# Reordering the first block of a fused scan, gated MLP and routed MoE kernel

## The chip, the cores and the metric

One core of one Trainium2 chip. The time is device microseconds of a run of the whole program, from the first instruction to the last and the little that lies around them. Three runs of the kernel before give 530.34 to 531.74 us, the median is 531.46 us.

## What is computed

Three layers follow each other. The first is a chunked linear attention with decay: 4 batches of 8 heads, 768 positions, head size 32, state size 16. The reference does it in chunks of 32 positions, cut to what matters:

```python
cum = np.cumsum(log_a_chunk)
M = (C @ B.T) * np.exp(cum_i - cum_j) * causal
y = M @ x + (C @ state) * np.exp(cum_i)
state = np.exp(sum(log_a_chunk)) * state + sum_j(B_j x_j * np.exp(cum_last - cum_j))
```

The second is a gated MLP on the 3072 tokens of 256 features, `(silu(x @ w_gate) * (x @ w_val)) @ w_out` with 1536 hidden features. The third picks one of 8 experts for each token, `relu(x @ w1[e]) @ w2[e]` with 1024 hidden features, scaled by the expert's probability.

## The kernel before

The attention is done in 24 units of 128 positions of one batch, all eight heads at once; four units make a block of 512 tokens, and there are six blocks. A unit u goes through these steps. `load` asks for its two tiles, `xbb` (x and B) and `cbd` (C, block by block on a diagonal). `weigh` multiplies x by a decay (line 278, on POOL or DVE). `scores_mm` makes the new states and the scores on PE (lines 291 and 297). `scores_m` masks the scores on DVE (line 305) and `states` carries the state on DVE and ACT (lines 315 to 327). `values_mm` multiplies on PE (lines 343 and 353). `values_out` scales by the decay `U` on DVE (lines 369 to 372) and rounds to fp32r on ACT (line 374). `values_low` takes the rounding's remainder on DVE (line 380). The decays `U` of a block come from `emit_d` (line 259, a product on POOL for the first two blocks) and `emit_u` (line 270, two products of 512 columns on PE, and line 271, two copies on ACT).

All products of the MLP are in fp32r with a high and a low part of both sides, so three products stand for one. The MLP's weights arrive as 64-bit words in 12 tiles f of 768 KB (`load_w`, line 391, three buffers) and are turned into fp32 by `decode(f, ...)`. Its parts are: 0 and "t", two passes on ACT (lines 403 and 406); "b" and "c", two passes on DVE over 768 columns (lines 412 and 416), which together are part 1; 2, the high part `wh`, on ACT (line 419); 3, the low part `wl`, on DVE or, for tile 0, on POOL (line 421).

The MLP of the first two blocks runs in 24 rounds i. A round makes the gate and the value products of one tile f on PE (`mlp1_mm`, line 441, 12 products `pg` and `pv` of 512 columns), the silu on ACT (line 448), the product on DVE (line 449) and its split into `hh` on ACT (line 455) and `hl` on DVE (line 456). The products with `w_out` (line 469) follow two rounds later. Between them stand the steps of the next units and the decoding of the next weight tile.

`first_block` writes the order of all of this out by hand, and every engine works through its own list in that order (`manual_schedule`). It first issues the loads, prepares the decays, takes units 0 to 3 in a loop (lines 836 to 872), in which PE is also given products that nobody reads (`keep_busy`, line 204), and then starts the rounds. DMAs are issued by SP (the loads) in the order of the text; a load waits on SP until its buffer is free, and what stands behind it waits too. The first MLP product needs units 0 to 3 and weight tile 0; round 1 needs weight tile 1.

The quoted numbers of lines are those of the kernel before.

## Time and profile before

| | |
|---|---|
| runs | 530.34 to 531.74 us, median 531.46 us |
| the profiled execution | 530.17 us, its span 528.4 us |
| PE busy | 505.0 us (96%) |
| DVE busy | 289.1 us (55%) |
| ACT busy | 219.5 us (42%) |
| POOL busy | 105.8 us (20%) |
| the chain that ended last | PE 76%, issue 11%, DVE 4%, POOL 3%, ACT 2%, DMA 1% |
| first MLP product | 24.40 us |

Busy times are sums over the whole span. The timeline has instructions in the order of time with their start, their length, the engine, the line, the tiles and, in brackets, how long the engine had been idle before and what released it. The window view has the busy time of each engine in a stretch. PE rows count passes, of which an fp32 product has two. The last slices of the span hold the loop over further expert tiles.

### The profile page before, as it was taken

To read this page: it belongs to the slowest core of one execution; us is meant where nothing else is said; L and a number is where in the kernel's file an instruction comes from. 1 tells how busy PE (TensorE), PEld (TensorE's weight loads), DVE (VectorE), ACT (ScalarE), POOL (GpSimd) and SP (SyncE) were. 2 spreads that over 40 slices of the span, in tenths; PEclk is the share of its full clock that TensorE was granted. 3 is DMA by queue.
4 is the path that set the end of the run, shared out by engine and by line. 5 is a ranking of instruction groups with operands and counts; after the bars stand their busy time and mean duration, and the time that the engine had idled before them with its cause. 6 is when DMAs were issued, how large, how long until landed. Compare 5 with 4: busy or idle time off the path is not lost.

```text
span 528.4 us, 11243 instructions
## 1 busy us (share of the span) xinstructions
PE 505.0 (96%) x4580; PEld 416.7 (79%) x4580; DVE 289.1 (55%) x631; ACT 219.5 (42%) x403; POOL 105.8 (20%) x127
## 2 busy tenths in 40 slices
PE   6889999999999999999999999999999999999990
PEld 3677787778788778888788778888899989999880
DVE  4998786944554544445444554455466564646320
ACT  4785575434333334233333332434454353534220
POOL 3200000220220130005000224211055426240220
PEclk9999999999999999999999999999999999999995
DMA  8954422011230312012100104234188544521100
GB/s 299 338 183 137 155 80 82 25 49 41 82 32 30 103 15 66 3 47 74 21 2 2 43 1 158 84 121 41 41 105 176 162 130 137 153 104 42 40 22 22
DMA packets 20694, 45.55 MB, mean 86 GB/s; under 512 B 4768, under 2 KB 8352, under 8 KB 20640
## 3 DMA queue, kind: packets, MB, share of 16 engines
q1 hardware_dynamic: 17424, 38.29, 26.2%
q0 software_dynamic: 3072, 6.41, 4.1%
q8 instruction: 37, 0.61, 0.6%
q14 instruction: 17, 0.14, 0.1%
q10 hardware_dynamic: 144, 0.11, 0.1%
HBM read 38.30 MB, written 6.50 MB: 85 GB/s over the span
## 4 chain that ended last, share of the span: by engine, by line
PE 76%; issue 11%; DVE 4%; POOL 3%; ACT 2%; DMA 1%; SPq 0%; POOLq 0%; DVEq 0%; ACTq 0%
PE py L469 19%; PE pg L441 18%; PE pv L441 18%; PE ph L758 7%; PE po L779 6%; PE pt L553 2%; POOL out L793 2%; PE pc L297 2%; PE py L353 1%; PE py L343 1%; PE pc L291 1%; DMA xbb<-in_xbb 1%; PE pu L270 1%; DVE wv L412 1%; PE px L747 1%
## 5 line engine op out<-in xcount | busy, mean ns | idle before, releaser
L441 PE MATMUL pg<-xt,wh 128*128 128x512 f32 x288 | 93.2, 404 | 0.3 <-ACT xt L374 0.2
L441 PE MATMUL pv<-xt,wh 128*128 128x512 f32 x288 | 90.4, 395 | 0.0
L449 DVE TENSOR_TENSOR h<-h,pv 128x512 f32<-128x512 f32 x72 | 49.4, 686 | 66.7 <-PE pv L441 55.6
L456 DVE TENSOR_TENSOR hl<-h,hh 128x512 fp32r<-128x512 f32 x72 | 50.2, 697 | 61.7 <-ACT hh L455 61.5
L758 PE MATMUL ph<-xt,hl 128*128 128x512 f32 x288 | 72.7, 394 | 0.0
L779 PE MATMUL po<-hl,hh 128*128 128x256 f32 x384 | 70.1, 283 | 0.0
L441 PEld LDWEIGHTS pv<-xt,wh 128*128 128x128 f32 x288 | 54.2, 188 | 12.8
L779 PEld LDWEIGHTS po<-hl,hh 128*128 128x128 f32 x384 | 60.3, 188 | 2.1
L455 ACT CAST hh<-h 128x512 fp32r<-128x512 f32 x72 | 44.6, 620 | 40.4 <-DVE h L449 40.4
L441 PEld LDWEIGHTS pg<-xt,wh 128*128 128x128 f32 x288 | 52.1, 188 | 11.6 <-ACT xt L374 0.6
L448 ACT ACTIVATE h<-pg 128x512 f32<-128x512 f32 x72 | 42.7, 593 | 41.7 <-PE pg L441 41.7
L614 POOL DMA_INDIRECT slots<-ids,si x24 | 26.0, 1081 | 168.4 <-DVE si L606 163.6
L758 PEld LDWEIGHTS ph<-xt,hl 128*128 128x128 f32 x288 | 51.7, 188 | 9.2
L469 PE MATMUL py<-hh,wh 128*128 128x512 f32 x144 | 58.7, 407 | 0.0
L441 PE MATMUL pg<-xt,wl 128*128 128x512 f32 x144 | 57.0, 396 | 0.3 <-DVE wl L421 0.3
L469 PE MATMUL py<-hl,wh 128*128 128x512 f32 x144 | 56.9, 395 | 0.0
L469 PE MATMUL py<-hh,wl 128*128 128x512 f32 x144 | 56.8, 394 | 0.0
L441 PE MATMUL pv<-xt,wl 128*128 128x512 f32 x144 | 56.8, 394 | 0.0
L779 PE MATMUL po<-hl,hl 128*128 128x256 f32 x192 | 53.9, 281 | 0.2 <-DVE hl L767 0.2
L767 DVE SCALAR_TENSOR_TENSOR hl<-ph,hh 128x512 fp32r<-128x512 f32 x48 | 33.0, 688 | 31.8 <-ACT hh L766 30.8
L766 ACT ACTIVATE hh<-ph 128x512 fp32r<-128x512 f32 x48 | 28.8, 600 | 41.4 <-PE ph L758 24.3
L779 PEld LDWEIGHTS po<-hl,hl 128*128 128x128 f32 x192 | 36.1, 188 | 0.4 <-DVE hl L767 0.4
(140 smaller groups left out, 669.6 us busy)
## 6 DMA issues: line engine op xcount, KB each, us to landing
eraw<-in_ew SPq DMA_DIRECT2D x24, 512.0 KB
wraw<-in_mw SPq DMA_DIRECT2D x12, 768.0 KB
xbb<-in_xbb SPq DMA_DIRECT2D x24, 256.0 KB
cbd<-in_cbd SPq DMA_DIRECT2D x24, 256.0 KB
yd<-yr SPq DMA_DIRECT2D x6, 528.0 KB
slots<-ids,si POOLq DMA_INDIRECT x24
xg<-yd,idx POOLq DMA_INDIRECT x24
out<-ob,idx POOLq DMA_INDIRECT x24
```

The source lines that it names most:

```text
L297: nc.tensor.matmul(out=r["pc"][g][32 * q:32 * q + 32, 0:256], lhsT=r["bt"][k, 32 * q:32 * q + 32], rhs=r["c"][k, q // 2].rearrange("p h i ...
L441: nc.tensor.matmul(out=t, lhsT=w[:, f, o:o + 128], rhs=xt[:, xp, k, cs], start=n == 0, stop=n == 5)
L448: nc.scalar.activation(out=h, in_=p[0], func=AF.Silu)
L449: nc.vector.tensor_tensor(out=h, in0=h, in1=p[1], op=ALU.mult)
L455: nc.scalar.copy(out=hh, in_=h)
L456: e.tensor_tensor(out=hl, in0=h, in1=hh.bitcast(F32), op=ALU.subtract)
L469: nc.tensor.matmul(out=yb[b][d][:, c:c + m], lhsT=w[:, f, o:o + 128], rhs=h, start=first and n == 0, stop=last and n == 2, skip_group_chec ...
L614: i = nc.gpsimd.indirect_dma_start(out=slots[0:E * upto], out_offset=bass.IndirectOffsetOnAxis(ap=si[:, s:s + 1], axis=0), in_=ids[g][:, o ...
L758: nc.tensor.matmul(out=p, lhsT=self.hl[:, w, o:o + 128], rhs=self.xt[:, xp, k], start=n == 0, stop=n == 5)
L766: nc.scalar.activation(out=hh, in_=p, func=AF.Relu)
L767: nc.vector.scalar_tensor_tensor(out=hl, in0=p, scalar=0.0, in1=hh.bitcast(F32), op0=ALU.max, op1=ALU.subtract)
L779: nc.tensor.matmul(out=self.po[s // 2][:, s % 2], lhsT=h[:, q], rhs=self.hl[:, w, o:o + DM], start=f == 0 and n == 0 and s % 2 == 0, stop= ...
```

## The change

Only `first_block`, `load` and part 3 of `decode` change. `load` can be issued by another engine, and part 3 can be divided over two engines by columns. In `first_block`:

- the small decay product `d2` is made before the constants of `setup_ones`, and `emit_d(0)` stands ahead of `weigh(1)` on POOL;
- `load(3)` moves from the first loads to ACT's queue, `load_w(1)` from there to the end of unit 1, `load_w(2)` and `load_w(3)` to units 2 and 3;
- `emit_u(1)` moves from unit 0 to unit 2; the products that nobody reads are 2, 2, 4 and 4 instead of 0, 4, 4 and 6 after the four units;
- the parts of `decode(0)` move one unit later; its low part is done in unit 3, 512 columns on DVE and 256 on POOL, instead of in unit 1 with all 768 on POOL;
- `decode(1)` keeps its ACT passes 0 and "t" in units 2 and 3, and its DVE passes and the high part move behind `scores_m(4)` and `states(4)`;
- `weigh(6)` on DVE moves from the head of round 0 to just before it.

The number of products of each line of PE stays as it was, but for line 204, which has 12 instead of 14.

```diff
--- before.py
+++ after.py
@@ -157,17 +157,17 @@
     v_t = {}
     s_t = {}
 
-    def load(u):
+    def load(u, e=nc.sync):
         if u >= NU or u in raw:
             return
         r = {}
         xbb = ap_.tile([128, 512], F32, name="xbb", tag="xbb", bufs=4)
-        nc.sync.dma_start(out=xbb, in_=I["xbb"][:, u])
+        e.dma_start(out=xbb, in_=I["xbb"][:, u])
         r["x"] = xbb[:, 0:DM].rearrange("k (h d) -> k h d", h=8)
         r["b"] = xbb[:, DM:DM + 128]
         r["bt"] = xbb[:, DM + 128:]
         r["c"] = ap_.tile([128, 2, 4, 64], F32, name="cbd", tag="cbd", bufs=4)
-        nc.sync.dma_start(out=r["c"].rearrange("p r h i -> p (r h i)"), in_=I["cbd"][:, u])
+        e.dma_start(out=r["c"].rearrange("p r h i -> p (r h i)"), in_=I["cbd"][:, u])
         raw[u] = r
 
     def setup_loads():
@@ -418,8 +418,10 @@
             elif part == 2:
                 nc.scalar.copy(out=wh[:, f], in_=wv_t[f].bitcast(F32))
             else:
-                low.tensor_tensor(out=wl[:, f], in0=wv_t.pop(f).bitcast(F32), in1=wh[:, f].bitcast(F32),
-                                  op=ALU.subtract)
+                v = wv_t.pop(f)
+                for e, k in ((low, slice(0, 768)),) if low is nc.vector else low:
+                    e.tensor_tensor(out=wl[:, f, k], in0=v[:, k].bitcast(F32), in1=wh[:, f, k].bitcast(F32),
+                                    op=ALU.subtract)
 
 
     HALF = NF // 2
@@ -812,29 +814,30 @@
         nc.sync.dma_start(out=at0[:, 2:], in_=I["at"][:, 2:])
         load(2)
         load_w(0)
-        load(3)
-        load_w(1)
         setup_ln(0, 2)
         setup_decay(0, 2)
         setup_cum(0, 1)
         weigh(0, nc.vector)
         scores_mm(0)
         cum_split(0, 1)
+        p = cum_ends_d(0, 1)
         setup_ones()
+        d = emit_d(0)
         weigh(1, nc.gpsimd)
-        d = emit_d(0)
-        p = cum_ends(0, 1, cum_ends_d(0, 1))
+        p = cum_ends(0, 1, p)
         scores_m(0)
         cum_store(0, 1, p)
         states(0)
         emit_u(0, d)
         cum_pairs(1, 8)
         setup_ln(2, NBLK)
-        decode(0, 0)
+        load(3, nc.scalar)
         d = emit_d(1)
         weigh(2, nc.gpsimd)
         for u in range(4):
             scores_mm(u + 1)
+            if u == 2:
+                emit_u(1, d)
             values_mm(u)
             if u == 1:
                 setup_decay(2, NBLK)
@@ -842,36 +845,38 @@
             if u < 3:
                 scores_m(u + 1)
                 states(u + 1)
-            if u in (0, 2):
-                decode(u // 2, "t")
+            if u == 2:
+                decode(1, 0)
             values_out(u)
             if u == 0:
-                emit_u(1, d)
+                decode(0, 0, "t")
+            if u == 1:
                 decode(0, "b")
-            if u == 1:
+            if u == 2:
                 decode(0, "c")
-            if u == 2:
-                decode(1, "b")
-            keep_busy((0, 4, 4, 6)[u])
+            if u == 3:
+                decode(1, "t")
+                silu_first()
+            keep_busy((2, 2, 4, 4)[u])
             values_low(u)
             load(u + 4)
             if u == 0:
                 weigh(3, nc.gpsimd)
             if u == 1:
+                load_w(1)
+                weigh(4, nc.gpsimd)
+            if u == 2:
                 load_w(2)
+                weigh(5, nc.gpsimd)
+                decode(0, 2)
+            if u == 3:
+                decode(0, 3, low=((nc.vector, slice(0, 512)), (nc.gpsimd, slice(512, 768))))
                 load_w(3)
                 nc.sync.dma_start(out=c2, in_=I["cst"][:, C1:C_END])
-                weigh(4, nc.gpsimd)
-                decode(0, 2)
-                decode(0, 3, low=nc.gpsimd)
-                decode(1, 0)
-            if u == 2:
-                decode(1, "c")
-                silu_first()
-                decode(1, 2)
-                weigh(5, nc.gpsimd)
         scores_m(4)
         states(4)
+        decode(1, 1, 2)
+        weigh(6, nc.vector)
         decode(1, 3)
         decode(2, 0, "t")
         load_w(4)
@@ -883,7 +888,7 @@
             b, f = q % 2, f + HALF * (q // 2)
             u = units.get(i)
             w = todo.get(i, NF)
-            if i + 1 in units and units[i + 1] > 4:
+            if i + 1 in units and units[i + 1] > 5:
                 weigh(units[i + 1] + 1, nc.vector if i < 16 else nc.gpsimd)
             if u == 7:
                 mlp1_down(*late.pop(0))
```

The rows below are as the built programs have them: engine by engine, line, operation, output and inputs, shape of the output.

POOL, from its first own row. `xw` is the weighed x of a unit, `du` the input to a block's decays `U`, `wl` the low part of weight tile 0. Before:

```order
L278 TENSOR_TENSOR xw<-xbb,W 128x256
L259 TENSOR_TENSOR du<-er,c_69 128x512 x2
L278 TENSOR_TENSOR xw<-xbb,W 128x256 x3
L421 TENSOR_TENSOR wl<-wv,wh 128x768
L278 TENSOR_TENSOR xw<-xbb,W 128x256
```

After:

```order
L259 TENSOR_TENSOR du<-er,c_69 128x512
L278 TENSOR_TENSOR xw<-xbb,W 128x256
L259 TENSOR_TENSOR du<-er,c_69 128x512
L278 TENSOR_TENSOR xw<-xbb,W 128x256 x4
L423 TENSOR_TENSOR wl<-wv,wh 128x256
```

The first `du` now stands ahead of the first `xw`, and the low part is a third as wide and the last of these.

DVE, from the third unit's last steps to the first rounds. `wv` is a weight tile's bits (L412 is "b", L416 is "c"), `y` and `z` a unit's values, `xt` its remainder, `mt` the masked scores, `sv` and `se` the states. Before, from "b" of tile 1 on:

```order
L412 SCALAR_TENSOR_TENSOR wv<-ha,wv 128x768
L380 TENSOR_TENSOR xt<-y_422,xt 128x2x128
L416 SCALAR_TENSOR_TENSOR wv<-wraw,wv 128x768
L369 TENSOR_TENSOR y_497<-py,U 128x192
L370 TENSOR_TENSOR z_498<-py,U 128x128
L371 TENSOR_TENSOR y_497<-py,U 128x64
L372 TENSOR_TENSOR y_497<-y_497,z_498 128x128
L380 TENSOR_TENSOR xt<-y_497,xt 128x2x128
L305 TENSOR_TENSOR mt<-pc,c_69 128x256 x2
L321 SCALAR_TENSOR_TENSOR sv<-se,eb,pc 128x64
L324 SCALAR_TENSOR_TENSOR se<-sv,eb,pc 128x64
L421 TENSOR_TENSOR wl<-wv,wh 128x768
```

After, from the fourth unit's remainder on:

```order
L380 TENSOR_TENSOR xt<-y_486,xt 128x2x128
L423 TENSOR_TENSOR wl<-wv,wh 128x512
L305 TENSOR_TENSOR mt<-pc,c_69 128x256 x2
L321 SCALAR_TENSOR_TENSOR sv<-se,eb,pc 128x64
L324 SCALAR_TENSOR_TENSOR se<-sv,eb,pc 128x64
L412 SCALAR_TENSOR_TENSOR wv<-ha,wv 128x768
L416 SCALAR_TENSOR_TENSOR wv<-wraw,wv 128x768
L278 TENSOR_TENSOR xw<-xbb,W 128x256
L423 TENSOR_TENSOR wl<-wv,wh 128x768
```

"b" and "c" of tile 1 stand behind `mt`, `sv` and `se` of the fifth unit, and 512 columns of tile 0's low part stand ahead of them. Ahead of `y_486` there is one such pass now, "c" of tile 0.

SP, the loads from the first weight tile on. Before:

```order
L391 DMA wraw<-in_mw 128x1536
L165 DMA xbb<-in_xbb 128x512
L170 DMA cbd<-in_cbd 128x512
L391 DMA wraw<-in_mw 128x1536
L165 DMA xbb<-in_xbb 128x512
L170 DMA cbd<-in_cbd 128x512
```

After:

```order
L391 DMA wraw<-in_mw 128x1536
L165 DMA xbb<-in_xbb 128x512
L170 DMA cbd<-in_cbd 128x512
L165 DMA xbb<-in_xbb 128x512
L170 DMA cbd<-in_cbd 128x512
L391 DMA wraw<-in_mw 128x1536
```

Before, the two loads behind the first weight tile are unit 3; after, they are units 4 and 5, and weight tile 1 stands behind both.

## Rows read from the trace of the kernel before

**Rows 1.** Windows: length; busy of PE, PEld, DVE, ACT, POOL; PE clock; DMA; GB/s.

```profile
28.00:32.00 4.00, 4.00 (x92) 3.09 (x76) 3.85 (x8) 3.45 (x7) 0.00 (x0) 1.00 0.32 72
32.00:36.00 4.00, 2.55 (x101) 2.15 (x101) 3.95 (x8) 2.30 (x5) 0.00 (x0) 1.00 0.67 264
60.00:80.00 20.00, 20.00 (x89) 16.21 (x88) 15.63 (x28) 15.12 (x29) 0.00 (x0) 1.00 0.34 106
```

**Rows 2.** Waits of PE over the whole span: total, times, longest.

```profile
PE pc L291 <- DVE mt L305: 1.5, 1, 1.5
PE pc L297 <- issue: 0.9, 1, 0.9
```

**Rows 3.** The chain that ended last, 50 to 60 us.

```profile
52.47 0.97 DVE wl L421
53.48 1.19 PE pg L441 x4
54.67 1.40 PE pv L441 x6
```

**Rows 4.** Timeline, the start: POOL, DVE and PE up to unit 1's scores.

```profile
5.32 0.30 DVE L226 TENSOR_TENSOR er<-er,eh 128x132 f32<-128x132 f32 x1
...
6.61 0.61 POOL L278 TENSOR_TENSOR xw<-xbb,W 128x256 f32<-128x256 f32 x1 [6.17 <-DMA xbb<-in_xbb]
...
7.18 2.17 POOL L259 TENSOR_TENSOR du<-er,c 128x512 fp32r<-128x512 f32 x2
...
8.27 1.22 PE L270 MATMUL pu<-du,r 128*128 128x512 f32 x2 [1.60 <-POOL du L259]
...
9.43 0.47 PE L291 MATMUL pc<-xw,xbb 64*32 64x64 f32 x16
```

**Rows 5.** Timeline of PE: scores of units 2 to 4, first product, later scores.

```profile
12.57 0.47 PE L291 MATMUL pc<-xw,xbb 64*32 64x64 f32 x16
...
16.37 1.16 PE L204 MATMUL pi<-r 128*128 128x512 f32 x4
...
19.99 0.34 PE L291 MATMUL pc<-xw,xbb 64*32 64x64 f32 x16
...
24.40 0.96 PE L441 MATMUL pg<-xt,wh 128*128 128x512 f32 x2 [0.21 <-ACT xt L374]
...
33.76 0.28 PE L291 MATMUL pc<-xw,xbb 64*32 64x64 f32 x7 [1.45 <-DVE mt L305]
```

**Rows 6.** Timeline of DVE, 20 to 28 us.

```profile
20.10 0.52 DVE L372 TENSOR_TENSOR y<-y,z 128x128 f32<-128x128 f32 x1
20.70 1.22 DVE L412 SCALAR_TENSOR_TENSOR wv<-ha,wv 128x768 int32<-128x768 int32 x1
...
22.17 0.94 DVE L416 SCALAR_TENSOR_TENSOR wv<-wraw,wv 128x768 int32<-128x768 int32 x1
...
23.64 0.27 DVE L372 TENSOR_TENSOR y<-y,z 128x128 f32<-128x128 f32 x1
24.38 0.42 DVE L380 TENSOR_TENSOR xt<-y,xt 128x256 fp32r<-128x256 f32 x1 [0.47 <-ACT xt L374]
...
25.89 0.95 DVE L421 TENSOR_TENSOR wl<-wv,wh 128x768 fp32r<-128x768 f32 x1
26.76 0.42 DVE L278 TENSOR_TENSOR xw<-xbb,W 128x256 f32<-128x256 f32 x1
27.68 0.96 DVE L412 SCALAR_TENSOR_TENSOR wv<-ha,wv 128x768 int32<-128x768 int32 x1 [0.50 <-ACT wv L406]
```

**Rows 7.** Timeline: SP, ACT and POOL on the weight tiles.

```profile
4.51 0.43 SPq L391 DMA_DIRECT2D wraw<-in_mw  x1
...
11.24 0.92 ACT L403 ACTIVATE ha<-wraw 128x768 f32<-128x768 f32 x1 [0.75 <-DMA wraw<-in_mw]
...
18.62 1.85 POOL L421 TENSOR_TENSOR wl<-wv,wh 128x768 fp32r<-128x768 f32 x1 [2.75 <-ACT wh L419]
...
23.15 0.83 ACT L419 CAST wh<-wv 128x768 fp32r<-128x768 f32 x1 [0.57 <-DVE wv L416]
```

## The prediction

> **What bounds the kernel now.** I read the page first: PE is busy for 96% of the span and holds 76% of the chain that ended last, so only a moment at which PE waits can be worth anything. The windows say where there are such moments: from 60 us on PE is busy for all 20 us of 20, while from 32 to 36 us it has 2.55 of 4 and DVE 3.95 of 4 [rows 1]. The waits of PE name one large one behind the start of the MLP, 1.45 us for DVE's masked scores [rows 2, 5]. The chain of work runs on DVE once more up to 53.48 us, and from there on PE alone [rows 3]. So the time is fixed by two things: when the first MLP product starts (24.40 us, [rows 5]), and whether DVE and ACT, which decode weights and serve the units beside it, then keep up. What comes out at 33.76 us, where PE is released by DVE, moves the rest of the program one for one. I therefore sum the change in two stretches: to the first product, and from there to that release.
>
> **Stretch one: to the first product.**
>
> 1. The decays first. Now POOL takes unit 1's weighing at 6.61 us, after waiting for its load, and only then the two decay products, 2.17 us for both; PE gets the first at 8.27 us after 1.60 us of idle time [rows 4]. The decays' input is ready when DVE is done with it, at 5.32 + 0.30 = 5.62 us. With the decay first on POOL it is done at about 5.65 + 1.08 = 6.73, and PE starts at about 6.75: 1.52 us earlier. The weighing behind it ends at 7.35 and is needed when the two 512-column products are through, 6.75 + 1.15 = 7.9; it is hidden by half a microsecond. Moving the small product d2 ahead of the constants gains nothing: PE is at scores until 6.3 anyway.
> 2. Units 1 to 2. The scores of unit 1 start at 9.43 - 1.52 = 7.9. Up to the scores of unit 2 the distance is 12.57 - 9.43 = 3.14 us now [rows 4, 5]; the two 512-column products in it (block 1's decays) give way to two others of the same size, so these start at 11.05.
> 3. Units 2 to 4. From there to unit 4's scores it is 19.99 - 12.57 = 7.42 us [rows 5]. Two of the four unread products go (1.16 us for four, so 0.58), the two of block 1's decays come (0.58): zero. Unit 4's scores start at 18.5.
> 4. To the first product it is 24.40 - 19.99 = 4.41 us now. In it DVE does "b" and "c" of tile 1, 1.22 and 0.94 us, ahead of unit 3's values [rows 6]; in their place it has one pass, "c" of tile 0 (0.95). That takes 1.2 us out: 3.2. The two unread products fewer are hidden, since PE waits for DVE and ACT there. First product at 21.7, **2.7 us earlier**.
> 5. What hides the rest. Unit 3 is asked for by ACT, two issues of some 0.4 us each behind its logarithm, at about 9 us. Now the load leaves SP earlier but stands behind weight tile 0, which took from 4.51 until 11.2 to land [rows 7]. I take it to land at about 12.5; unit 3's scores, which need it, cannot start before 11.05 + 3.14 = 14.2, so it has 1.7 us to spare. Tile 1's load now stands on SP behind unit 5's, which waits for unit 1's values; it is issued at about 13.8. ACT wants it at about 18, ahead of unit 2's rounding on the same queue. The nearest row has 6.7 us from issue to landing for such a tile, with a full queue around it; 768 KB at the 264 GB/s of a window [rows 1] are 3.0 us. Between these I take 4.2 us, nearer the low end because few loads stand ahead by then, so that it lands at 18.0 and costs nothing, and keep 20.5 as the late end.
> 6. Tile 0's low part on two engines: POOL's 1.85 us become about 0.62 for a third of the columns, beginning as soon as the high part is done; DVE gets 0.95 x 512 / 768 = 0.63 us in stretch two.
>
> [...] DVE's last step on a unit's values took 0.52 us at 20.10 and 0.27 at 23.64 [rows 6]; at 20.10 POOL was at its low part, which ran until 20.47 [rows 7]. [...]
>
> **Stretch two: from the first product to the release of PE by DVE.** Now DVE takes 33.76 - 24.38 = 9.38 us from unit 3's remainder to that release [rows 5, 6], all but idle only for 0.50 us. Behind the change it does the same list and in addition:
>
> 7. 0.63 us of tile 0's low part (point 6).
> 8. "b" and "c" of tile 1, 0.96 and 0.95 us without disturbance: 1.9 us.
> 9. A wait. Tile 1's high part is made by ACT (0.83 us) after "c", and the low part on DVE needs it; before, it had long been there. Unit 6's weighing (0.42) lies beside it: +0.4 us. Then tile 2's two ACT passes (0.92 and about 0.9) come behind the high part, and DVE has the low part (0.95) beside 1.8 us of them: 0.85 us of waiting instead of 0.50: +0.35 us.
>
> So it takes 9.4 + 0.63 + 1.9 + 0.75 = 12.7 us: **3.3 us longer**. Starting from 21.7 it ends at 34.4, 0.65 us later than now. PE sees this as follows: round 1 starts at about 29, as now, because round 0's silu on ACT stands behind tile 1's high part and tile 2's passes, and PE idles before it for some 2.5 us; the next scores wait again for DVE.
>
> **Sum.** -2.7 + 3.3 = +0.6 to +0.7 us on the profiled execution of 530.17 us, so 530.8. The median of the runs is 1.29 us above that execution; on it the forecast is 531.46 + 0.65, rounded to **532.1 us**: no change that a measurement could tell, 0.3% being 1.6 us. Unknown costs: PE's wait of 0.9 us for nothing the profile shows [rows 2] may not come back, and PE's faster clock may come earlier. [...] If the upper level comes 2 us sooner, half of these is won, -1.0. At the other end stand the late landing of point 5 (+2.0 at most) and the 0.6 us of the port.
>
> **Rivals.**
>
> - *DVE has room after all (faster).* If stretch two hid its additions beside PE's work, the 2.7 us would stay but for DVE's 0.63: 531.46 - 2.1 = 529.4 us. For it: DVE is busy for only 55% of the span. Against: it has 3.95 us of 4 where it matters [rows 1], and the 1.45 us of PE's wait are there before anything is added. It decides from 1.0 us of slack upwards; the trace shows 0.50.
> - *Weight tile 1 is late (slower).* Its place on SP is behind two loads that wait for PE and for their buffers. ACT then stands before the tile's first pass, and unit 2's rounding, unit 2's remainder on DVE and unit 3's values stand behind it. Each microsecond of landing after about 18.2 is one on both stretches. At the 6.7 us of tile 0 it lands at 20.5: +2.3 on top of the forecast, 534.4 us. It counts as slower from 19.2 us on. For it: that is the one row that times such a load. Against: the DMA queue is emptier by then.
> - *The clock falls (slower).* PE idles for some 2.5 us before round 1 and again before the next scores. In the trace it came through a wait of 1.45 us at 33.76 without losing its clock, since six products take 1.40 us afterwards [rows 3]. At the lower level each six would take 2.8, and one round (two sixes) behind the idle time would cost 2.8 us: 534.9. [...]
> - *It does nothing.* The counts of PE's lines are the same but for two unread products, so no product that counts is saved; all is order. If stretch two's waits of point 9 fall into time that is idle anyway, gain and loss cancel, and the time is 531.5.
>
> **Chances.** The forecast has 0.69, DVE with room 0.10, the late tile 0.14, the fallen clock 0.03, nothing 0.04. Same is 0.69 + 0.04 = 0.73, slower 0.14 + 0.03 = 0.17, faster 0.10. The range: from 532.1 down by the 1.9 us of the unknowns on that side, to some 530.0; upwards by 2.0, the late tile's most likely part, to 534.0.
>
> **What would show it.** Right: a first PE decay product near 6.75 us, a first MLP product between 21 and 22.5, a PE wait of 2 us or more ahead of round 1, then the scores released by DVE near 34.4, and the same stretch from there to the end. Wrong: round 1 starting 4.6 us behind round 0 as now; ACT waiting for a weight tile's DMA near 18 us; six products taking 2.8 us after 29 us; or any difference that comes up behind 55 us.

## The result and the profile after

| | median us | runs | lowest to highest |
|---|---|---|---|
| before, same series | 530.75 | 8 | 530.34 to 531.74 |
| after | 533.32 | 8 | 532.19 to 535.73 |

The ratio is 1.0052, with a 95% interval of 1.0039 to 1.0066: 2.6 us slower. That is inside the forecast's range, but outside the 0.3% that it called no change. The profiled executions are 530.17 us before and 532.19 us after (the fastest of its eight), with spans of 528.4 and 530.0 us.

First PE's timeline, whose rows answer to [rows 4, 5]. The columns are as there: start, duration, engine, line, operation, tiles, count, and in brackets the idle time ahead and what ended it.

```profile
6.95 0.40 PE L238 MATMUL pe<-d,r 128*128 128x32 f32 x1 [0.46 <-DVE r L215]
7.25 1.19 PE L270 MATMUL pu<-du,r 128*128 128x512 f32 x2
...
11.51 0.47 PE L291 MATMUL pc<-xw,xbb 64*32 64x64 f32 x16
...
17.80 0.34 PE L291 MATMUL pc<-xw,xbb 64*32 64x64 f32 x16
19.59 0.67 PE L297 MATMUL pc<-cbd,xbb 64*32 64x256 f32 x16 [1.45 <-issue]
...
22.34 0.95 PE L443 MATMUL pg<-xt,wh 128*128 128x512 f32 x2 [0.27 <-ACT xt L374]
...
29.37 0.72 PE L443 MATMUL pg<-xt,wh 128*128 128x512 f32 x2 [1.97 <-ACT h L450]
...
34.96 0.28 PE L291 MATMUL pc<-xw,xbb 64*32 64x64 f32 x7 [1.58 <-DVE mt L305]
```

The reader sees the trade of the forecast. The first MLP product comes 24.40 - 22.34 = 2.06 us earlier. PE then idles 1.97 us ahead of round 1, which it did not do before, and the release of PE by DVE comes 34.96 - 33.76 = 1.20 us later. The first stretch ends 0.64 us later than its forecast of 21.7, and it has two waits nobody counted, at 6.5 and at 18.1 us.

The timelines of the other engines say what stands behind the waits (rows for [rows 4, 6, 7]):

```profile
5.83 1.07 DVE L215 CAST r<-c 128x128 fp32r<-128x128 f32 x1
...
5.77 1.04 POOL L259 TENSOR_TENSOR du<-er,c 128x512 fp32r<-128x512 f32 x1 [5.34 <-DVE er L226]
...
13.69 0.42 SPq L391 DMA_DIRECT2D wraw<-in_mw  x1
...
18.76 0.89 ACT L403 ACTIVATE ha<-wraw 128x768 f32<-128x768 f32 x1 [1.40 <-DMA wraw<-in_mw]
...
19.98 0.43 DVE L380 TENSOR_TENSOR xt<-y,xt 128x256 fp32r<-128x256 f32 x1 [1.02 <-ACT xt L374]
20.97 0.36 DVE L369 TENSOR_TENSOR y<-py,U 128x192 f32<-128x192 f32 x1 [0.57 <-PE py L353]
...
22.67 0.69 DVE L423 TENSOR_TENSOR wl<-wv,wh 128x512 fp32r<-128x512 f32 x1
...
24.44 0.95 DVE L412 SCALAR_TENSOR_TENSOR wv<-ha,wv 128x768 int32<-128x768 int32 x1
25.43 0.96 DVE L416 SCALAR_TENSOR_TENSOR wv<-wraw,wv 128x768 int32<-128x768 int32 x1
...
27.28 0.96 DVE L423 TENSOR_TENSOR wl<-wv,wh 128x768 fp32r<-128x768 f32 x1 [0.56 <-ACT wh L419]
28.87 0.96 DVE L412 SCALAR_TENSOR_TENSOR wv<-ha,wv 128x768 int32<-128x768 int32 x1 [0.62 <-ACT wv L406]
```

Weight tile 1, asked for at 13.69, is there 5.0 us later, and ACT waits 1.40 us for it. DVE's remainder of unit 2 at 19.98 then waits 1.02 us, because ACT's rounding stands behind the tile. It is not the tile that sets the first product here, though: at 20.97 DVE stands 0.57 us more, for PE's values of unit 3, which come behind PE's wait at 18.1 us. Behind the first product DVE does the three additions of the forecast's points 6 to 8 (0.69, 0.95 and 0.96 us) and stops twice for ACT.

In one cut, from the first product to the release DVE's list took 33.76 - 24.40 = 9.36 us before and 34.96 - 22.34 = 12.62 after. It got 3.26 us longer for a start that was 2.06 us earlier. That is the +1.20. Some 0.4 us more come up behind the release: from there to the end of the span it is 494.6 us before and 495.0 after. They come among the expert tiles, from some 420 us on, and in no other profile: the twelve below have 494.4 to 494.7, so the release does move the rest one for one. Another 0.4 us lie around the span: 530.17 - 528.4 = 1.8 us before, 532.19 - 530.0 = 2.2 after.

Not explained by this profile is that the median is +2.57 us and the runs spread over 3.5 us, where before's spread over 1.4.

### The profile page after: what moved, and what is told of

It reads as the page before. It is cut to its first block, busy times and chain, and to the rows that moved or that the text cites. A ratio compares the mean times of both kernels' runs of the same rounds, so it can differ in the third digit from the quotient of the medians.

```text
span 530.0 us, 11238 instructions
## 1 busy us (share of the span) xinstructions
PE 505.1 (95%) x4578; PEld 416.1 (79%) x4578; DVE 290.6 (55%) x632; ACT 219.5 (41%) x403; POOL 104.9 (20%) x127
## 4 chain that ended last, share of the span: by engine, by line
PE 77%; issue 11%; DVE 5%; POOL 2%; ACT 2%; DMA 1%; SPq 0%; POOLq 0%; ACTq 0%
PE py L471 19%; PE pg L443 18%; PE pv L443 18%; PE ph L760 7%; PE po L781 6%; PE pt L555 2%; PE pc L297 2%; POOL out L795 2%; PE py L353 1%; PE py L343 1%; PE pc L291 1%; DVE wv L412 1%; PE pu L270 1%; PE px L749 1%; POOL xg L719 1%
## 5 line engine op out<-in xcount | busy, mean ns | idle before, releaser
L443 PEld LDWEIGHTS pv<-xt,wh 128*128 128x128 f32 x288 | 54.1, 188 | 13.5 <-DVE h L451 0.9
```

What stands on the lines that cost most here:

```text
L443: nc.tensor.matmul(out=t, lhsT=w[:, f, o:o + 128], rhs=xt[:, xp, k, cs], start=n == 0, stop=n == 5)
```

## Theories

- **A.** DVE's list behind the first product sets the release; its additions and its waits for ACT are the loss.
- **B.** Weight tile 1 lands too late. What the median shows beyond the profile is a tile that usually lands later than in the profiled run.
- **C.** TensorE's clock falls in PE's new idle time, and that is most of the loss.

All versions ran in five rounds beside before, whose median in the four series was 530.41, 530.38, 530.36 and 530.36 us. This table holds what the profiles of all of them say; "stretch two" is the release less the first product, the last column the median less before's of the same series.

| version | tile 1 landed | first product | release | stretch two | median |
|---|---|---|---|---|---|
| before | 14.4 | 24.40 | 33.76 | 9.36 | 0 |
| after | 18.7 | 22.34 | 34.96 | 12.62 | +2.57 |
| a_again | 20.0 | 23.64 | 35.98 | 12.34 | +2.61 |
| decode_first | 20.6 | 23.99 | 35.97 | 11.98 | +1.88 |
| low_pool | 19.7 | 24.15 | 36.17 | 12.02 | +2.26 |
| tile_early | 13.1 | 22.46 | 35.05 | 12.59 | +2.04 |
| old_loads | 14.7 | 23.13 | 35.73 | 12.60 | +2.07 |
| old_first | 14.3 | 22.90 | 34.88 | 11.98 | +1.48 |
| no_bc | 21.1 | 24.47 | 35.74 | 11.27 | +0.73 |
| act_tile | 17.7 | 23.66 | 35.84 | 12.18 | +1.67 |
| loads_act | 17.9 | 24.30 | 33.66 | 9.36 | +0.50 |
| du_only | 14.1 | 24.02 | 33.37 | 9.35 | -0.38 |
| du_all | 14.1 | 24.12 | 32.91 | 8.79 | -0.98 |
| unit3_sp | 19.3 | 22.75 | 35.35 | 12.60 | +2.30 |

## Experiments

### The changed kernel once more (a_again)

No edit.

> The changed kernel once more, with another trace. Theory A (DVE's list: the work put behind the fifth unit's states, and the waits for ACT around it, outweigh the earlier start): again 0.3 to 0.6% slower than before, PE released by DVE's masked scores at 34.5 to 35.5 us, and every six products behind 29 us in 1.4 us. Theory B (weight tile 1 lands late): the release moves one for one with the landing of tile 1, which ACT waits for. Theory C (PE's clock falls in the idle time ahead of round 1 in some runs): six products take 2.8 us somewhere between 29 and 34 us if this trace is of such a run.

533.02 us (532.59 to 534.47), ratio 1.0049 (1.0031 to 1.0067). Its profile is of a more usual run than the first. First its timeline:

```profile
19.98 0.92 ACT L403 ACTIVATE ha<-wraw 128x768 f32<-128x768 f32 x1 [2.46 <-DMA wraw<-in_mw]
...
20.36 0.67 PE L297 MATMUL pc<-cbd,xbb 64*32 64x256 f32 x16 [2.29 <-issue]
...
21.86 0.36 DVE L369 TENSOR_TENSOR y<-py,U 128x192 f32<-128x192 f32 x1 [0.21 <-PE py L353]
...
23.64 1.05 PE L443 MATMUL pg<-xt,wh 128*128 128x512 f32 x2
...
32.50 1.22 PE L443 MATMUL pv<-xt,wh 128*128 128x512 f32 x2 [0.22 <-DVE h L451]
...
35.98 0.25 PE L291 MATMUL pc<-xw,xbb 64*32 64x64 f32 x3 [0.42 <-DVE mt L305]
```

And its windows, with the columns of [rows 1], the granted clock in front of the last two:

```profile
22.00:24.00 2.00, 2.00 (x5) 1.39 (x6) 1.53 (x6) 1.08 (x2) 0.73 (x1) 0.50 0.59 180
...
26.00:28.00 2.00, 2.00 (x56) 1.48 (x58) 1.71 (x3) 0.70 (x2) 0.00 (x0) 1.00 0.63 239
...
32.00:34.00 2.00, 1.78 (x5) 1.21 (x5) 2.00 (x6) 1.44 (x3) 0.00 (x0) 0.50 0.54 129
```

The tile took 6.4 us from its issue at 13.60 and ACT waited 2.46 us, so it is late as B has it. But again DVE stood last for PE's values, 0.21 us: PE, which had waited 2.29 us at 18.07, set the first product, with the tile close behind. That product is 1.3 us later than in the first profile, and stretch two is not longer. C is seen too, twice: at 22 and at 32 us the granted clock is at 0.50, and two products at 32.50 took 1.22 us, for 0.73 in the first profile. The first fall, in the unread products, held the first product some 0.3 us longer but not DVE: counted from DVE's remainder of unit 3 (23.35) the release comes 12.63 us later, as in the first profile (12.64 from 22.32). The second fall moved nothing either: PE's wait ahead of the release is 0.42 us in place of 1.58, so the slower products went into a wait for DVE that was there anyway.

### Tile 1's decode ahead of unit 4's masked scores (decode_first)

```diff
+        decode(1, 1, 2)
         scores_m(4)
         states(4)
-        decode(1, 1, 2)
```

> Undoes one part: both DVE passes of tile 1 and its high part stand ahead of the fifth unit's masked scores and states again, all else as changed. Theory A: DVE's two waits for ACT (0.56 and 0.62 us) shrink, round 1 starts 0.6 to 0.9 us sooner, PE is released at 33.9 to 34.4, and the time is 0.6 to 1.0 us below the changed kernel's, 532.3 to 532.7. Theory B: the tile is as late as before, no change, 533.3. Theory C: PE idles about 0.7 us less; the same or up to 2 us less.

532.29 us (530.70 to 532.76), ratio 1.0027 (1.0017 to 1.0038), 0.7 us below the changed kernel in the same series. Stretch two has 11.98 us in place of 12.6. Unit 4's masked scores and states now lie where DVE waited 0.56 us for the high part, and the next wait is shorter:

```profile
28.59 0.95 DVE L423 TENSOR_TENSOR wl<-wv,wh 128x768 fp32r<-128x768 f32 x1
29.89 0.96 DVE L412 SCALAR_TENSOR_TENSOR wv<-ha,wv 128x768 int32<-128x768 int32 x1 [0.35 <-ACT wv L406]
```

A step that only reorders DVE's list gives its microseconds back, as A says. The release itself, 35.97, is not at the forecast 33.9 to 34.4, because the tile landed at 20.6 in this profile and the first product came at 23.99.

### The low part on POOL alone (low_pool)

```diff
-                decode(0, 3, low=((nc.vector, slice(0, 512)), (nc.gpsimd, slice(512, 768))))
+                decode(0, 3, low=((nc.gpsimd, slice(0, 768)),))
```

> Undoes one part: tile 0's low part is all on POOL again (768 columns), all else as changed. Theory A: DVE's list is 0.69 us shorter, PE is released 0.6 us sooner, 532.7. The first product's third partner may come as late as 22.7, which costs nothing as the release counts. Theory B and C: no change, 533.3, within 0.3 us.

532.67 us (532.52 to 533.31), ratio 1.0040 (1.0026 to 1.0055). Two rows of the timeline stand side by side:

```profile
21.71 1.80 POOL L423 TENSOR_TENSOR wl<-wv,wh 128x768 fp32r<-128x768 f32 x1 [4.06 <-ACT wh L419]
...
21.87 1.79 DVE L372 TENSOR_TENSOR y<-y,z 128x128 f32<-128x128 f32 x1
```

A DVE step that takes 0.27 us undisturbed [rows 6] took 1.79 us and ended 0.15 us behind POOL's. So the split avoids most of a stop of 1.5 us on DVE at the price of 0.69 us of DVE work (stretch two is 12.02 here), and comes out about even: of the 0.35 us by which this median is below the changed kernel's in the same series, 0.3 lie around the span (below). The time is the 532.7 that A gave, but not by A's way: the release, 36.17, came later and not 0.6 us sooner.

### Tile 1 asked for early (tile_early)

```diff
             values_low(u)
+            if u == 0:
+                load_w(1)
             load(u + 4)
...
-                load_w(1)
                 weigh(4, nc.gpsimd)
```

> Undoes one part: weight tile 1 is asked for at the end of unit 0 instead of unit 1, ahead of the fifth unit's loads. Theory A: ACT's wait of 1.40 us for the tile goes, and with it up to 1.0 us of DVE's idle time at 19 us, but PE's own wait in unit 4's scores holds the first product; 0 to 0.6 us less than the changed kernel, 532.7 to 533.3. Theory B: the whole loss goes, 530.7 or below. Theory C: no change.

532.45 us (531.60 to 533.75), ratio 1.0034 (1.0020 to 1.0048). The queue took the issue at 4.96 us, and the tile landed at 13.08. ACT no longer waits for it. But unit 3 landed at 14.85, and POOL waited for that:

```profile
14.98 1.57 POOL L278 TENSOR_TENSOR xw<-xbb,W 128x256 f32<-128x256 f32 x2 [5.70 <-DMA xbb<-in_xbb]
```

Release and stretch two are those of the changed kernel's first profile. The median is 0.6 us below a_again's; what a late unit 3 took back of B's worth this run can't tell, since the late tile was exchanged for it.

### Both loads in their old place (old_loads, old_first)

```diff
         load_w(0)
+        load(3)
+        load_w(1)
...
-        load(3, nc.scalar)
...
-                load_w(1)
                 weigh(4, nc.gpsimd)
```

old_first has the edit of decode_first besides.

> The changed kernel with the loads of unit 3 and of weight tile 1 back in their old places, on SP's queue right behind weight tile 0; all else as changed. Theory A with B (DVE's added work sets the release of PE, at 35.0 us where the tile is there in time; what the runs without a profile lose beyond that is the tile landing 5 to 7 us after its late issue): the tile lands near 14.5, ACT waits for no load, unit 3 is there before its scores, release 34.6 to 35.1, and the time is 531.7 to 532.1, with a small spread as before's. B alone (the late tile is all of the loss): the time of before, 530.5. C (a clock that falls in PE's idle time is most of the loss): 533 as the changed kernel, with its spread.

> The two old loads, and tile 1's second decode ahead of unit 4's masked scores and states. A with B: DVE's two passes on the tile and ACT's high part come earlier, so DVE no longer waits 0.56 us for the high part, and round 1 comes sooner: release 33.9 to 34.5, time 530.9 to 531.4, the best of the series so far, but not faster than before by what can be told. B alone: 530.5, as the run with the old loads. C: PE idles less ahead of round 1, 532.0.

532.45 us (531.72 to 532.77), ratio 1.0032 (1.0022 to 1.0041), and 531.86 us (531.12 to 532.02), ratio 1.0019 (1.0011 to 1.0028). The spread is before's again. tile_early, with the tile early and unit 3 late, had a spread of 2.15 us, so the wide spread is not tile 1's late landing alone. Against a_again and decode_first, their likes with late loads, the two gain 0.5 and 0.4 us. The second, whose release of 34.88 and time came later than its forecast, is the best version that has all of the change's other parts, and still 1.5 us above before, 0.4 of it around the span.

The time of old_loads is above what A with B gave it, and its first product is 0.8 us later than after's although no load is late. Some 0.3 us of that is DVE's last step on unit 3's values, which took 0.55 us beside POOL's part of the low part and 0.28 in after. The rest is PE. The timeline:

```profile
15.64 0.69 PE L193 MATMUL pe<-c,at 128*128 128x132 f32 x4 [1.85 <-DVE y L372]
...
21.76 0.74 POOL L423 TENSOR_TENSOR wl<-wv,wh 128x256 fp32r<-128x256 f32 x1 [2.37 <-ACT wh L419]
...
22.10 0.55 DVE L372 TENSOR_TENSOR y<-y,z 128x128 f32<-128x128 f32 x1
...
23.13 0.95 PE L443 MATMUL pg<-xt,wh 128*128 128x512 f32 x2 [0.55 <-ACT xt L374]
...
35.73 0.28 PE L291 MATMUL pc<-xw,xbb 64*32 64x64 f32 x7 [1.59 <-DVE mt L305]
```

The releaser that is named is not the likely one: DVE's L372 ended at 15.13, and after does the same products without a wait for it. Other records fit better: the view of the DMA queues lists, in a window, packets of the kind "instruction" (queue, kind: packets, MB, share of 16 engines). First old_loads, 12 to 14.5 us; then after, 9.5 to 12 us; then before, 13 to 14.5 us:

```profile
q1 hardware_dynamic: 393, 0.96, 99.4%
q8 instruction: 1, 0.02, 2.3%
```

```profile
q10 hardware_dynamic: 241, 0.45, 49.4%
q1 hardware_dynamic: 175, 0.40, 43.0%
q8 instruction: 1, 0.02, 4.1%
```

```profile
q1 hardware_dynamic: 292, 0.56, 98.2%
q8 instruction: 1, 0.02, 3.9%
```

By the packet records this one packet of 16 KB (before's queue q8 has 37 of the kind over the span, 0.61 MB) ran 13.12 to 14.05 us in old_loads, 13.40 to 14.34 in before and 10.12 to 11.77 in after, and the next one 17.30 to 18.27 in after. PE started again 1.59 us behind the end of the first in old_loads, 1.56 in before (its row "15.90 ... [0.85 <-issue]"), and 1.32 us behind the second in after: its wait of 1.45 us at 18.14. The fourteen profiles have such stops at two places of PE's program alone: at the products of L186 and L193 near 14 us, and at L297 of unit 4's scores near 19. In all fourteen the restart of such a stop is 1.3 to 1.6 us behind a packet's end, so these packets are read here as PE's own code and called code packets below; no view names the engine that they are for. The view counts them in the same share of 16 engines as the loads of q1 and q10 (4.1% in after's window). The first of them starts at 12.8 to 13.4 us in the five profiles with both loads in their old place on SP, and at 10.1 to 12.2 in the nine others. Full engines alone do not explain that: in after's window they are at some 96% too, half of it from ACT's queue (q10). What the packet waits for no run shows.

### Less work on DVE (no_bc)

```diff
-        decode(1, 1, 2)
+        decode(1, 2)
         weigh(6, nc.vector)
```

> The changed kernel without DVE's two passes 'b' and 'c' of weight tile 1 (its exponent and sign are left out, so that part of the first MLP's weights is not the reference's); 1.9 us of DVE work less between the first product and the release, nothing else. A: the release falls by 1.5 to 1.9 us against the changed kernel with the same landing of the tile, to 33.1 to 33.6, and the time is 531.0 to 531.5 or less. B (the late tile holds all up through ACT): under 0.5 us of gain, 532.5. C: PE's idle time ahead of round 1 gets shorter by about 1.5 us; if that saves the clock, more than 1.9 us are won and the spread shrinks.

The run leaves out the passes "b" and "c" of tile 1. 531.11 us (530.30 to 532.70), ratio 1.0014 (1.0003 to 1.0025): 1.9 us below the changed kernel's 533.02 of the series before, as A said. It was a run with a very late tile that was profiled:

```profile
21.11 0.90 ACT L403 ACTIVATE ha<-wraw 128x768 f32<-128x768 f32 x1 [3.38 <-DMA wraw<-in_mw]
...
24.47 0.96 PE L443 MATMUL pg<-xt,wh 128*128 128x512 f32 x2 [1.87 <-ACT xt L374]
...
27.98 0.96 DVE L423 TENSOR_TENSOR wl<-wv,wh 128x768 fp32r<-128x768 f32 x1 [1.00 <-ACT wh L419]
```

So its release, 35.74, does not show the gain; stretch two, 11.27 us, does: 1.35 us shorter, and 0.44 us of the rest went into a longer wait for ACT (1.00 against 0.56).

### Tile 1 asked for by ACT (act_tile)

```diff
         load(3, nc.scalar)
+        load_w(1, nc.scalar)
...
-                load_w(1)
                 weigh(4, nc.gpsimd)
```

> The changed kernel with one thing moved: weight tile 1 is asked for by ACT, right behind unit 3, at about 9.7 us in place of 13.7. It tells the tile's landing from the load of PE's code: every run so far in which unit 3 and tile 1 were asked for early (on SP, at 5 to 6 us) shows the first 16 KB load of PE's code ending near 14.0 and PE standing still until 1.3 to 1.6 us after that, and every run in which they were asked for late shows it ending by 11.8 and PE not standing there. A with B and with the code load as a second reason of the time at which the first MLP product starts: the tile lands by 16.5, ACT does not wait for it, the code load ends by 12.5 and PE has no idle time near 14, first product 22.3 (2.1 earlier than before), release 35.0 (1.2 later), time 531.6 to 532.0 with a small spread. If the code load has nothing to do with the loads ahead of it: PE idles near 14 as with the old loads, first product 23.1, release 35.7, 532.4. C: 533 with the spread of the changed kernel.

532.03 us (531.82 to 532.47), ratio 1.0030 (1.0019 to 1.0042). The first code packet ended at 11.70 us and PE did not stand at 14, as expected if the code waits behind SP's loads. (What is said there of every run has one exception: in decode_first the packet ended at 12.64 and PE stood 0.67 us at 13.5.) The rest of the forecast failed in the profile: the tile took 7.5 us and landed at 17.66, and the second code packet ended at 18.89, behind its loads; its timeline and two of its windows:

```profile
20.26 0.68 PE L297 MATMUL pc<-cbd,xbb 64*32 64x256 f32 x16 [2.23 <-issue]
...
21.88 0.36 DVE L369 TENSOR_TENSOR y<-py,U 128x192 f32<-128x192 f32 x1 [2.07 <-PE py L353]
...
35.84 0.28 PE L291 MATMUL pc<-xw,xbb 64*32 64x64 f32 x7 [0.65 <-DVE mt L305]
```

```profile
22.00:24.00 2.00, 2.00 (x5) 1.54 (x6) 1.53 (x6) 1.20 (x2) 0.00 (x0) 0.50 0.67 220
...
32.00:34.00 2.00, 2.00 (x6) 1.36 (x5) 1.97 (x6) 1.44 (x4) 0.00 (x0) 0.50 0.66 135
```

ACT's wait for the tile is all but gone (0.23 us), and the first product is no earlier than a_again's (23.66 against 23.64): PE restarted at 20.26, and DVE stood 2.07 us for its values. Here PE's stop alone holds the first product. The spread is small, with the clock falling in the same two places as in a_again, and with the mean granted clock of the run under 0.9885 in 4 of 7. So the clock alone does not make the spread.

### Unit 3 alone back on SP (unit3_sp)

```diff
         load_w(0)
+        load(3)
...
-        load(3, nc.scalar)
```

> The changed kernel with unit 3's load alone back on SP in its old place; weight tile 1 stays late. It is to tell which of the two moved loads goes with the lowered clock: of the runs with both loads in their old place (the version with the old loads, the one with tile 1's decode first as well, the decays alone and the version that should beat both) 2 of 45 show a mean granted clock under 0.9885; of those with unit 3 on ACT's queue (the changed kernel in two series and the seven other versions, early tile or late) 50 of 81. If unit 3's place on ACT's queue is what matters: few such runs here, and the time is set by the tile's landing (5 to 7 us after its issue) and DVE's work, 532.2 to 532.7 with a spread under 1.5 us. If the tile's lateness is what matters: half of the runs or more, 532.5 to 533.5.

The count quoted there was wrong: it is 44 of 72 runs and six other versions, not 50 of 81. Measured: 532.66 us (532.04 to 533.52), ratio 1.0050 (1.0036 to 1.0063); the mean granted clock is under 0.9885 in 3 of 5 runs. So unit 3's queue alone is not what goes with the lowered clock; with tile_early (5 of 9), either load out of its old place is enough, and only both in place give 2 of 45. The numbers of runs are small, and what in them lowers it stays open. In the profile the tile landed at 19.31, the clock was at 0.50 from 30 to 32 us, PE's wait ahead of the release was 0.74 us, and stretch two was 12.60, the same as with the clock up.

### The parts alone, on the kernel before (loads_act, du_only)

loads_act moves the two loads of before to ACT's queue, behind the logarithm of the later blocks. du_only has the change's first part:

```diff
+        p = cum_ends_d(0, 1)
         setup_ones()
-        weigh(1, nc.gpsimd)
         d = emit_d(0)
-        p = cum_ends(0, 1, cum_ends_d(0, 1))
+        weigh(1, nc.gpsimd)
+        p = cum_ends(0, 1, p)
```

> The kernel before with its loads of unit 3 and of weight tile 1 moved to ACT's queue, two steps later, and nothing else: that part of the change alone. If the code load stands behind the loads ahead of it, it ends by 12.5 in place of 14.3 and PE's 0.85 us of idle time near 15 goes, but DVE and ACT, with the decode of tile 0, set the first product as before: it starts 0 to 0.4 us earlier or, with ACT's issues of some 1.2 us ahead of tile 0's first pass, up to 0.5 later; time 530.2 to 530.9. Rival (loads asked for later are harmful by themselves): 531.4 and more, with ACT waiting for tile 1.

> The kernel before with the decays' order alone changed (d2 ahead of the constants, du ahead of unit 1's weighing on POOL). A: PE gets its first decay product 1.0 to 1.5 us earlier and unit 1's scores too, but DVE and ACT, which decode weight tile 0 from its landing at 11.2 on, and the stretch behind it stay as they are, so that most of it is waited away: the first MLP product comes 0 to 0.7 us earlier, the time is 530.4, within 0.5. Rival (each microsecond at the head is one at the end): 529.2. Its profile also shows whether DVE's cast beside POOL's decay takes 1.07 us here as well, as in the changed kernel, in place of 0.22.

loads_act: 530.86 us (529.78 to 532.39), ratio 1.0009 (0.9998 to 1.0019), which can't be told from no change. The code packet ended at 12.68 and the 0.85 us of PE's wait went, as expected; the first product came only 0.10 us earlier. Its runs come in two kinds: six at a mean clock of 0.989 and over, 529.78 to 530.86 us, and five at 0.984 to 0.986, 531.10 to 532.39. Here a lowered clock goes with about 1.1 us of time. Runs under 0.9885 have a median 1.25 us above the others in before (8 of 85 runs) and 1.4 us in the changed kernel's first series (6 of 8), but -0.3 to +0.6 us in decode_first, low_pool, tile_early, no_bc, act_tile and unit3_sp.

du_only: 530.00 us (529.68 to 530.67), ratio 0.9990 (0.9982 to 0.9999). DVE's cast beside POOL's decay takes 1.07 us here as well, and PE's first decay product came at 7.62, 0.65 us earlier, not 1.0 to 1.5; the first product 0.38 us earlier, and the release too. Nothing of it was lost behind.

### A version that beats both (du_all)

du_only with three steps moved:

```diff
-            if u in (0, 2):
-                decode(u // 2, "t")
+            if u == 1:
+                decode(0, "b")
+            if u == 2:
+                decode(1, "t")
             values_out(u)
             if u == 0:
+                decode(0, "t")
                 emit_u(1, d)
-                decode(0, "b")
...
             keep_busy((0, 4, 4, 6)[u])
+            if u == 3:
+                scores_m(4)
             values_low(u)
...
-        scores_m(4)
         states(4)
```

> A version that should beat both, from what the runs say of DVE: the kernel before, with the decays' order of the change (which gave 0.4 us alone), and three steps of DVE and ACT moved into gaps of DVE: unit 2's masked scores and states ahead of tile 0's 'b' (which waits 0.72 us for ACT's pass there), ACT's pass 't' behind unit 0's rounding, and unit 4's masked scores ahead of unit 3's remainder (which waits 0.47 us for ACT). No step is added. A (DVE's time without work between 11 us and the release is what can be won): release 0.8 to 1.2 us earlier than before, at 32.6 to 33.0, time 529.2 to 529.7, ratio 0.998. Rival (PE's code load and its idle time near 14 and 20 us set the first product now): the same as with the decays alone, 530.0.

529.38 us (528.87 to 530.74), ratio 0.9979 (0.9970 to 0.9989): faster than before by 1.0 us and, against a_again, than the changed kernel by 3.6. DVE's masked scores now fill the 0.47 us in which it waited for ACT [rows 6], and the release moves:

```profile
23.55 0.74 DVE L305 TENSOR_TENSOR mt<-pc,c 128x256 f32<-128x256 f32 x2
24.21 0.41 DVE L380 TENSOR_TENSOR xt<-y,xt 128x256 fp32r<-128x256 f32 x1
...
32.91 0.28 PE L291 MATMUL pc<-xw,xbb 64*32 64x64 f32 x7 [0.79 <-DVE mt L305]
```

The first product, 24.12, is no earlier than du_only's 24.02; stretch two is 0.56 us shorter. It was won with DVE's idle time and the order of its list, without a later load and without a step more. Which of the three moved steps gave how much was not tried.

## Why the prediction was half right

The sign and the mechanism were right: an earlier start, paid for by a longer list on DVE. The size was not: +0.65 us was forecast and +2.57 measured, and 0.73 of the chance lay on "no change". That 533.32 is inside the range is in part luck: the range stands on 531.46, the median of three runs, and on the 530.75 of the series its upper end would be 533.3. Of the forecast's own signs of being wrong two came: ACT waited for the tile until 18.7 us, and 0.4 us came up behind 55.

Rows for point 1, before and then a_again (after's are above, at 5.77, 5.83 and 6.95):

```profile
5.54 0.22 DVE L215 CAST r<-c 128x128 fp32r<-128x128 f32 x1
```

```profile
6.84 0.72 DVE L216 CAST r<-c 128x256 fp32r<-128x256 f32 x1
...
7.71 1.19 PE L270 MATMUL pu<-du,r 128*128 128x512 f32 x2 [0.34 <-DVE r L216]
```

Step by step:

- **Points 7 to 9, stretch two: right.** 12.7 us were forecast, counted from DVE's remainder of unit 3. Counted so, the six profiles with an unchanged list (after, a_again, tile_early, old_loads, act_tile, unit3_sp) have 12.61 to 12.64, and the two that only reorder it 12.00. Neither the late tile nor the lowered clock made it longer. The parts are right too: 0.69 us for 0.63, 1.9 for 1.9, waits of 0.56 and 0.62 ahead of tile 1's and tile 2's passes for 0.4 and 0.85.
- **Point 1: wrong by 0.5 us.** Forecast 6.75, measured 7.25 (7.6 to 7.7 in most versions). The sum let POOL's decay alone release PE. PE's products there also need DVE's two casts of the constants, of which the forecast says only that moving d2 ahead of them "gains nothing". The first cast had 0.22 us before, with POOL idle, and has 1.07 in all twelve profiles with the new order, ending 0.1 us behind POOL's decay in after. The second has 0.28 there, and 0.72 beside POOL's weighing in the eight profiles with 7.6 to 7.7. Whether d2's place or POOL's order brings them together no version separates. The forecast looked at such a meeting of DVE and POOL for the low part only (0.52 us for 0.27).
- **Points 2 and 3: right and better.** 3.14 us to unit 2's scores as forecast (8.37 to 11.51). From there to unit 4's scores it took 6.29 us for 7.42 and they came at 17.80, for 18.5: before's wait of 0.85 us at 15.90 was gone, and the other 0.28 go with products that got faster sooner (PE's 16 products of L297 took 1.10 us at 12.79 before and 0.80 at 11.73 after, against 0.64 later in both). For its -1.0 us the forecast has a clock that rises to an upper level; no run shows such a rise, as the granted clock reads 1.00 in both kernels' windows from 4 to 20 us, and these 0.28 us are what the runs show in its place.
- **Point 4: wrong.** 3.2 us were forecast from there to the first product, and 17.80 to 22.34 is 4.54. 1.45 us of it are PE's wait ahead of 19.59, of which the prediction had listed 0.9 as a wait that "may not come back". It came back longer, and 2.29 us long in a_again, and in both profiles of the changed kernel it set the first product.
- **Point 5: the mis-sized term.** Tile 1 was taken at 4.2 us from issue to landing, and kept at 6.7 as the late end. In the six profiles with it on SP behind unit 5's loads it took 5.0, 6.4, 7.0, 5.5, 7.0 and 5.4 us (after, a_again, decode_first, low_pool, no_bc, unit3_sp). In the last four of them DVE did not stand for PE's values: there the tile set the first product, which came 3.4 us behind the landing in decode_first, no_bc and unit3_sp. Unit 3 landed at 13.5, for 12.5, and cost nothing. The row that timed such a load was the better guide than the bandwidth of a window.
- **Point 6: right in after, not in the others.** 0.74 us on POOL and 0.69 on DVE, and in after POOL's part met no step of DVE that it slowed. The forecast's sum had nothing for such a meeting. In a_again, decode_first, old_loads, old_first, no_bc and unit3_sp POOL's part began later or DVE's last step on unit 3's values sooner, and that step took 0.42 to 0.72 us in place of 0.28: up to 0.44 us on the first product, within the 0.6 that the forecast had named. No run shows the port to which it puts these 0.6 us; what the runs show in its place is the longer step, by those 0.44 us at most, and by 1.5 in low_pool.
- **Left out: the time around the span.** It is 1.8 to 1.9 us in before, du_only, du_all, loads_act, low_pool and no_bc, and 2.2 us in the eight others, by the medians of their runs. Those eight have 632 instructions on DVE; the rest have 631 or 630. The split's second piece is that instruction, but no_bc has the split as well. What takes the 0.4 us was not tried.

So on the median: +1.2 us from the two stretches as first profiled, 0.4 around the span, and a rest of about 1 us. In a_again it is a later first product. The profiles show three things that make it late: PE's stop at unit 4's scores (2.29 us in a_again), tile 1's landing (5.0 to 7.0 us behind its issue), and POOL's part beside DVE's last step (up to 0.44 us). The lowered clock goes with the slow runs in before and after, but it moved the release in none of the three profiles that have it, so whether it makes a run late or only comes with a PE that waits stays open. How the rest divides in the runs without a profile was not settled; the old loads gave 0.4 to 0.5 us of it back, with before's spread. One profile does not carry its median here: in the versions with a moved load the two differ by up to 1.4 us (releases against medians, in the table), in the others by 0.4 at most.

The rivals: *weight tile 1 is late* happened as written, from 19.2 us on, in five of those six profiles, though in a_again PE was later still; it should have had a larger chance. *The clock falls* happened in three profiles; its price of 2.8 us, an estimate at half the speed of [rows 3], did not, since behind round 1 it ended in PE's wait for DVE (0.42 to 0.74 us in place of 1.6). (Half the speed fits [rows 4, 5], with two products in 1.22 us and four in 1.16, and a_again's two products in 1.22 us for 0.73 at 0.50.) (That the clock came through the wait at 33.76 is shown by the window of 32 to 36 us [rows 1], with 1.00, and not by the products at 53 us that the forecast gave.) Idle time ahead of round 1 alone did not bring the fall: the same 1.96 or 1.97 us of it was followed by 0.50 in act_tile and unit3_sp, and by 1.00 in after, old_loads and tile_early, so more decides than this wait. *DVE has room* is refuted by no_bc: with 1.9 us less work on DVE the time fell by 1.9, of which 0.3 lie around the span, and stretch two by 1.35.

## What to carry to other kernels

Where an engine that feeds PE sets the end of a stretch, add up that engine's list from its first to its last step, as durations plus waits: that sum held within 0.1 us. An earlier start is kept only if the list behind it gets no longer: du_only kept all of its 0.4 us, the change gave 3.26 for 2.06. Ahead of that stretch, ask what else an instruction needs besides the input that was moved, take for a load that moves later the longest row of its kind rather than bytes over bandwidth, and ask of each DVE step what POOL does in the same moment. Fill the waits of the busy engine with steps it has to do anyway, before steps are added to it.

## What the hardware showed that was not expected

- PE stood still near packets of 16 KB that the view of the DMA queues calls "instruction"; that they are its own code is a reading, which no view shows. At the scores of unit 4 it stood 0.5 to 2.3 us in every profile but tile_early's and the two with the old loads, at the same instruction, and started 1.3 to 1.6 us after a packet's end; the profile calls that "issue". In seven profiles it stood near 14 us as well, where the profile may name an engine that had long been done.
- DVE's cast of 128 columns took 1.07 us beside POOL's 1.04, and 0.22 alone; a DVE sum of 128 columns took 1.79 beside POOL's 1.80, and 0.27 alone.
- One instruction more on DVE went with 0.4 us more around the span.
